# The gradient transposed on TensorE in the head, two spectral pieces a step in the first group, and eight b tiles at the front of pass two

## The chip, the cores and the metric

The kernel runs on one core of a Trainium2 chip. The time is the device time of one execution in microseconds (us), as a median over runs; every run told here is of the fast state. Runs of one kernel on one chip scatter by up to 9 us (the kernel before took 1568.8 to 1577.8 us in 11 runs on one chip), so each comparison uses the runs of the kernel before that were made in the same rounds. Times inside an execution come from its trace, one for each kernel and two for the changed one; the two traces of the changed kernel differ by 1.9 us at the end of pass one and by 2.4 us in pass two, so a difference of that size between two traces proves nothing by itself. Engines: PE is TensorE, ACT is ScalarE, DVE is VectorE, POOL is GpSimd, SP is SyncE, which here only issues transfers. The granted clock of PE is given as a share of full speed.

## The reference, cut to what matters

Forward and backward pass of a gated sum of two branches over x with S = 2048 rows and D = 576 columns (bf16):

```python
g = sigmoid((x * gate_w).sum(-1, keepdims=True))
a = irfft2(rfft2(x) * (w_r + 1j * w_i))              # spectral branch
b = (gelu(x @ w_gate) * (x @ w_up)) @ w_down         # F = 4608
out = g * a + (1 - g) * b
# returned: out and the gradients of x, w_r, w_i, w_gate, w_up, w_down, gate_w for grad_out
```

Both branches read the same x. The gradient `grad_out` is needed in two layouts: natural (rows on partitions, tile `dB`) and transposed (columns on partitions, tile `dOT`).

## The kernel before

It has three stages. The **head** loads x, transposes it on PE chunk by chunk, and does the first two stages of the spectral transform for 16 row tiles. **Pass one** walks through 18 groups of 256 hidden columns, 8 steps each: matmuls H (`z` for the gradient, `xy` for gate and up), elementwise work on ACT and DVE, weight gradients W of the group before, and, in between, "pieces" of the spectral transforms. **Pass two** reads the stored hidden activations back with transposing transfers and computes b and the gradient of x.

The loads stand in one queue, that of SP (`LD`), and so do the stores of the head:

```python
for k in range(4):
    load_x(4 * k)
do_s = [dram.tile([4, P, 5 * P], BF16, name=f"do_s{k}") for k in range(4)]
for k in range(4):
    src = do_v[:, 4 * k:4 * k + 4, :].rearrange("p t d -> t p d")
    LD.dma_start(do_s[k][:, :, 0:D], src)            # staging copy, HBM to HBM
    LD.dma_start(do_s[k][:, :, D:], src[:, :, 512:D])
wts = {0: load_w(0)}
for k in range(4):
    LD.dma_start_transpose(dOT[:, :, 4 * k:4 * k + 4, :]..., do_s[k]...)
...
# second stage of a row tile t
Vt = unit([2, DF], name="Vt")                        # one of 19 shared buffers
V.tensor_copy(Vt[:], vps[:, :, :DF])
LD.dma_start(dst[t], Vt[:])                          # stored on the same queue
```

A step of pass one, and the pace of the pieces (`n` pieces done by the half step `h`; a `gap` in the list of pieces is an empty one, and `Vp` is a tile that the middle pieces load back from what the first ones stored):

```python
fft_until(want(step, 0))        # pieces of the first half; PSUM tile pf, one buffer
pts = H_mm(g, tp)               # z (every second step) and xy
tiles = H_ew1(g, tp, pts)       # ACT: da, q, xb, hu;  DVE: s, s, q, q
fft_until(want(step, 1))        # pieces of the second half
H_sig(tiles)
...
H_ew2(g, tp, tiles)
...
if h <= 2 * NT:                                      # group 0
    n = max(0, 3 * (h - 1) // 2)
```

In pass two `g` and `u` are the two halves of the gradient of x for a row tile (they share an accumulator), `b` is the down projection:

```python
jobs = [("g", t) for t in range(3)] + [("b", t) for t in range(6)] + [("u", t) for t in range(3)] + [("b", 6)]
for t in range(3, T):
    jobs += [("g", t), ("u", t)] + ([("b", t + 4)] if t + 4 < T else [])
...
for i, (kind, t) in enumerate(jobs):
    if i > 1 and wT_loads:
        load_wuT(*wT_loads.pop(0))                   # six transposing loads, jobs 2 to 7
```

## Time and profile before

The time is 1572.4 us. The prediction below shows and reads the profile's lines; this is the summary:

| stretch | from, us | length, us | what the trace shows |
|---|---|---|---|
| head, first part | 0 | 44.5 | PE busy 34.4 |
| hole | 44.5 | 19.1 | PE busy 0.29, ACT 0.64, DVE 0; buffers of Vt wait for their stores |
| head, rest | 63.6 | 14.3 | clock 0.62 of full |
| group 0 | 77.9 | 74.4 | PE busy 53.0 |
| groups 1 to 17 | 152.3 | 973.5 | PE-bound, but one group 6 us longer than its neighbours |
| pass two | 1125.8 | 444.7 | PE-bound, but for the b tiles in front |

The trace's span is 1570.5 us. "First z" below is the first z matmul, the start of group 0; the end of group 0 is z of step 8; pass two begins with the first matmul into `acc`.

### The profile page before, as it was taken

The numbers are of one execution on the slowest core, as the hardware profiler recorded it, in microseconds if no ns is written. First come the engines' busy times: TensorE is split into PE (matmuls) and PEld (weight loads), VectorE is DVE, ScalarE is ACT, GpSimd is POOL, SyncE is SP. The second block draws the span as 40 slices with busy tenths as digits, with TensorE's granted clock in tenths as the row PEclk, the third lists the DMA queues.
The fourth block names the chain that finished last, engine by engine and source line by source line (L and its number), as shares of the span: only waits on it lengthen the run. The fifth ranks groups of instructions, "written<-read, shape, count | busy, mean of one in ns | idle before, by whom it ended". The sixth has DMA issues, their size and how long they took to land.

```text
span 1570.5 us, 30102 instructions
## 1 busy us (share of the span) xinstructions
PE 1482.8 (94%) x11762; PEld 1080.0 (69%) x11886; DVE 823.7 (52%) x2168; ACT 708.8 (45%) x1357; POOL 22.5 (1%) x51
## 2 busy tenths in 40 slices
PE   7377999899999999999999999999998999999998
PEld 5234666566676666677767776766876777777776
DVE  6246767687888887656665665677112212121210
ACT  5145666576666666666666666666000000000000
POOL 0000000000000000000000000000000000000000
PEclk9689999999999999999999999999999999999999
DMA  3642333443544445344334454364999978777873
GB/s 122 156 154 74 104 110 110 144 131 117 149 142 138 132 117 166 98 117 118 101 111 118 121 118 122 102 157 122 266 191 207 207 156 170 156 166 158 172 149 70
DMA packets 518671, 217.47 MB, mean 138 GB/s; under 512 B 320128, under 2 KB 511616, under 8 KB 518528
## 3 DMA queue, kind: packets, MB, share of 16 engines
q1 hardware_dynamic: 515088, 209.80, 54.4%
q0 software_dynamic: 1632, 4.72, 1.1%
q8 instruction: 93, 1.52, 0.4%
q10 hardware_dynamic: 1808, 1.02, 0.2%
q14 instruction: 50, 0.41, 0.1%
HBM read 44.39 MB, written 97.33 MB: 90 GB/s over the span
## 4 chain that ended last, share of the span: by engine, by line
PE 68%; issue 23%; SPq 5%; DVE 1%; ACT 1%; POOL 1%; DMA 1%; POOLq 0%; DVEq 0%; ACTq 0%
PE wps L413 16%; PE xy L330 16%; PE wps L396 9%; PE z L319 8%; PE pf L666 3%; PE acc L870 3%; PE xy L327 2%; PE wps L424 2%; PE acc L912 2%; PE z L323 1%; SPq L246 1%; PE pf L453 1%; SPq L247 1%; SPq L250 1%; PE pf L650 1%
## 5 line engine op out<-in xcount | busy, mean ns | idle before, releaser
L330 PE MATMUL xy<-wgu,xT 128*128 128x512 bf16 x1028 | 257.4, 381 | 13.5 <-issue 10.4
L912 PEld LDWEIGHTS <-pin 128*128 128x128 bf16 x2304 | 225.4, 98 | 58.3 <-DMA pin<-scr 1.6
L413 PEld LDWEIGHTS <-xn 128*128 128x128 bf16 x2304 | 225.2, 98 | 35.5 <-issue 0.2
L330 PEld LDWEIGHTS <-xT 128*128 128x128 bf16 x1152 | 101.3, 98 | 143.5 <-issue 42.4
L341 ACT ACTIVATE da<-z,omg 128x256 bf16<-128x256 f32 x288 | 121.0, 473 | 103.6 <-PE z L323 103.6
L345 DVE TENSOR_SCALAR s<-q 128x512 bf16<-128x512 bf16 x144 | 42.2, 293 | 212.5 <-ACT q L342 212.2
L342 ACT ACTIVATE q<-xy 128x512 bf16<-128x512 f32 x144 | 86.0, 597 | 148.7 <-PE xy L330 148.7
L396 PE MATMUL wps<-dB,A 128*128 128x288 bf16 x1152 | 151.7, 288 | 0.0
L870 PE MATMUL acc<-wd_all,pin 128*128 128x288 bf16 x1152 | 145.3, 288 | 6.5 <-DMA pin<-scr 3.5
L912 PE MATMUL acc<-wuT,pin 128*128 128x288 bf16 x1152 | 143.4, 286 | 1.3 <-DMA pin<-scr 1.3
L319 PE MATMUL z<-wdT,dOT 128*128 128x256 bf16 x1152 | 140.9, 277 | 3.2 <-DVE Vt L475 3.2
L912 PE MATMUL acc<-wgT,pin 128*128 128x288 bf16 x1152 | 143.4, 286 | 0.0
L870 PEld LDWEIGHTS <-pin 128*128 128x128 bf16 x1152 | 113.3, 98 | 36.6 <-DMA pin<-scr 4.3
L396 PEld LDWEIGHTS <-A 128*128 128x128 bf16 x1152 | 113.6, 99 | 33.2
L413 PE MATMUL wps<-dHg,xn 128*128 128x256 bf16 x1152 | 131.7, 273 | 0.0
L413 PE MATMUL wps<-dHu,xn 128*128 128x256 bf16 x1152 | 131.3, 273 | 0.0
L319 PEld LDWEIGHTS <-dOT 128*128 128x128 bf16 x1152 | 114.0, 99 | 19.7 <-issue 3.8
L922 ACT COPY f32t<-acc 128x576 f32<-128x576 f32 x16 | 10.2, 639 | 250.5 <-PE acc L912 250.5
L924 DVE SCALAR_TENSOR_TENSOR f32t<-gwf,dlog,f32t 128x576 f32<-128x576 f32 x16 | 13.1, 818 | 179.7 <-ACT f32t L922 179.7
L353 ACT ACTIVATE om<-s 128x512 bf16<-128x512 bf16 x144 | 91.9, 638 | 15.1 <-DVE s L346 14.9
L354 ACT ACTIVATE s<-s 128x512 bf16<-128x512 bf16 x144 | 90.7, 630 | 4.6
L344 ACT CAST hu<-xy 128x512 bf16<-128x512 f32 x144 | 86.8, 603 | 0.0
(179 smaller groups left out, 1770.7 us busy)
## 6 DMA issues: line engine op xcount, KB each, us to landing
scr<-A SPq DMA_DIRECT2D x144, 128.0 KB
scr<-dHg SPq DMA_DIRECT2D x144, 128.0 KB
scr<-dHu SPq DMA_DIRECT2D x144, 128.0 KB
out_dram<-dw SPq DMA_DIRECT2D x67, 128.0 KB
wd_all<-in_B_w_down_dram SPq DMA_DIRECT2D x3, 1728.0 KB
out_dram<-dwd SPq DMA_DIRECT2D x34, 144.0 KB
scr_p<-Vt SPq DMA_DIRECT2D x32, 144.5 KB
Vp<-scr_p SPq DMA_DIRECT2D x16, 289.0 KB
```

What stands on the lines that cost most here:

```text
L319: nc.tensor.matmul(zt[0][:, t % 2, (t - t0) // 2, :], lhsT=dOT[:, ci, t, :], rhs=wdT[:, ci, :], start=(t < t0 + 2 and ci == 0), stop=False)
L330: nc.tensor.matmul(xy[:, tt, :], lhsT=xT[:, ci, t0 + tt, :], rhs=wgu[:, ci, :], start=False, stop=(ci == 3))
L341: nc.scalar.activation(da[:, tt, :], da_ps[:, tt, :], ACT.Copy, scale=omg32[:, t0 + tt:t0 + tt + 1])
L342: nc.scalar.activation(q[:], hg, ACT.Square)
L344: nc.scalar.copy(hu[:], hu_ps)
L353: nc.scalar.activation(om[:], s[:], ACT.Sigmoid, scale=-2.0 * C_GELU)
L354: nc.scalar.activation(s[:], s[:], ACT.Sigmoid, scale=2.0 * C_GELU)
L396: nc.tensor.matmul(wps[:, :288], lhsT=tl(0, t)[:, fch * P:(fch + 1) * P], rhs=dB[:, t, h * 288:(h + 1) * 288], start=(t == 0), stop=(t == ...
L413: nc.tensor.matmul(wps[:, cc, :], lhsT=xn[:, t, (c0 + cc) * P:(c0 + cc + 1) * P], rhs=tl(k, t), start=(t == 0), stop=(t == T - 1))
L666: nc.tensor.matmul(yps[:, h, :288], lhsT=Z[:, lc, c, :], rhs=tb.At[lc][:, c, h * 288:(h + 1) * 288], start=(n == 0), stop=(n == 5))
L870: nc.tensor.matmul(bps[:, h, :288], lhsT=At[:, r, :], rhs=wd_all[:, fc, h * 288:(h + 1) * 288], start=(fc == 0), stop=(fc == NFC - 1))
L912: nc.tensor.matmul(xps[:, h, :288], lhsT=src[:, r, :], rhs=wT[:, h * 288:(h + 1) * 288], start=(k == 1 and f0 + r == 0), stop=(k == 2 and ...
```

## The change

The intent was to take the gradient's staging and its DMA transposes out of the queue by transposing on PE from `dB`, which pass one needs anyway; to have one spectral piece a half step in group 0; and to give pass two more b tiles before the first u tile needs `wuT`. The diff, cut:

```diff
-    do_s = [dram.tile([4, P, 5 * P], BF16, name=f"do_s{k}") for k in range(4)]
     for k in range(4):
-        src = ...
-        LD.dma_start(do_s[k][:, :, 0:D], src)
-        LD.dma_start(do_s[k][:, :, D:], src[:, :, 512:D])
+        load_do(4 * k)
     wts = {0: load_w(0)}
-    for k in range(4):
-        LD.dma_start_transpose(dOT[...], do_s[k][...])
 ...
-    def x_chunk(t0):
+    def tchunk(src, dst, t0):          # 16 + 8 PE transposes, 3 copies
 ...
         if t % 4 == 2 and t < 14:
-            x_chunk(t + 2)
+            tchunk(xn, xT, t + 2)
+        if t >= 9 and t % 2 == 1:
+            tchunk(dB, dOT, 2 * (t - 9))
 ...
-    fft = at + fg + [gap] * 3 + mid[:-2] + ...
+    fft = at + fg + [gap] * 5 + mid[:-2] + ...
 ...
-    slot0 = 3 * (2 * NT - 1) // 2
+    slot0 = 2 * NT - 1
 ...
-            n = max(0, 3 * (h - 1) // 2)
+            n = max(0, h - 1)
 ...
-        for t0 in range(0, T, 4):      # in early_loads, step 1
-            load_do(t0)
 ...
-    jobs = ... [("b", t) for t in range(6)] + [("u", t) for t in range(3)] + [("b", 6)]
+    jobs = ... [("b", t) for t in range(8)] + [("u", t) for t in range(3)] + [("b", 8)]
     for t in range(3, T):
-        jobs += [("g", t), ("u", t)] + ([("b", t + 4)] if t + 4 < T else [])
+        jobs += [("g", t), ("u", t)] + ([("b", t + 6)] if t + 6 < T else [])
```

More of the change, by code (lines that the diff above doesn't have):

```diff
@@ L242 @@
         load_x(4 * k)
-    do_s = [dram.tile([4, P, 5 * P], BF16, name=f"do_s{k}") for k in range(4)]
     for k in range(4):
-        src = do_v[:, 4 * k:4 * k + 4, :].rearrange("p t d -> t p d")
-        LD.dma_start(do_s[k][:, :, 0:D], src)
-        LD.dma_start(do_s[k][:, :, D:], src[:, :, 512:D])
+        load_do(4 * k)
     wts = {0: load_w(0)}
-    for k in range(4):
-        LD.dma_start_transpose(dOT[:, :, 4 * k:4 * k + 4, :].rearrange("d c t p -> d c (t p)"),
-                               do_s[k][:].rearrange("t p d -> (t p) d"))
     gwb = res.tile([P, D], BF16, name="gwb")
@@ L284, in x_chunk @@
                     if c < 4:
-                        nc.tensor.transpose(tp_[:, 0, j, tt, :], xn[:, t0 + tt, c * P:(c + 1) * P], ident[:])
+                        nc.tensor.transpose(tp_[:, 0, j, tt, :], src[:, t0 + tt, c * P:(c + 1) * P], ident[:])
                     else:
                         for r in (LO, HI):
-                            nc.tensor.transpose(tp_[r, 0, 0, tt, :], xn[:, t0 + tt, 512:D], ident[:])
-            o = xT[:, cs[0]:cs[0] + len(cs), t0:t0 + 4, :]
+                            nc.tensor.transpose(tp_[r, 0, 0, tt, :], src[:, t0 + tt, 512:D], ident[:])
+            o = dst[:, cs[0]:cs[0] + len(cs), t0:t0 + 4, :]
             i = tp_[:, 0, 0:len(cs)]
@@ L687 @@
     build_D(nc, tb, unit, res)
-    x_chunk(0)
+    tchunk(xn, xT, 0)
     run_late(tb)
@@ L711 @@
     mid = mid_units()
-    fft = at + fg + [gap] * 3 + mid[:-2] + [load_At] + pa + mid[-2:] + [gap] * 2 + ia[:-4] + pb + ia[-4:] + ib
+    fft = at + fg + [gap] * 5 + mid[:-2] + [load_At] + pa + mid[-2:] + [gap] * 2 + ia[:-4] + pb + ia[-4:] + ib
     fft_pos = [0]
@@ L809, in pin @@
         return tl
-    jobs = [("g", t) for t in range(3)] + [("b", t) for t in range(6)] + [("u", t) for t in range(3)] + [("b", 6)]
+    jobs = [("g", t) for t in range(3)] + [("b", t) for t in range(8)] + [("u", t) for t in range(3)] + [("b", 8)]
     for t in range(3, T):
-        jobs += [("g", t), ("u", t)] + ([("b", t + 4)] if t + 4 < T else [])
+        jobs += [("g", t), ("u", t)] + ([("b", t + 6)] if t + 6 < T else [])
     seq = [("bgu".index(kind), t, f0) for kind, t in jobs for f0 in range(0, NFC, FCB)]
```

## The prediction

> **What bounds the kernel now.** I read the page first. Its second part, engines in 40 slices, says that PE is at 9 tenths in nearly every slice except the first four, and that its clock was not granted in slices two and three:
>
> ```profile
> PE   7377999899999999999999999999998999999998
> PEclk9689999999999999999999999999999999999999
> ```
>
> A slice is 1570.5/40 = 39.3 us, so whatever is to be gained lies mostly before 157 us. The view of windows (us; busy time and count of each engine; PE clock; DMA share; GB/s) cuts that stretch at its events: head up to the stall, stall, rest of head, first half of group 0, second half, then groups of 8 steps.
>
> ```profile
> 0.00:44.50 44.50, 34.43 (x284) 22.29 (x284) 27.52 (x69) 23.92 (x39) 3.57 (x17) 1.00 0.39 121
> 44.50:63.60 19.10, 0.29 (x3) 0.18 (x3) 0.00 (x0) 0.64 (x1) 0.00 (x0) 0.55 0.92 207
> 63.60:77.90 14.30, 9.85 (x117) 6.21 (x117) 7.11 (x22) 5.24 (x11) 0.00 (x0) 0.62 0.50 110
> 77.90:117.90 40.00, 29.33 (x160) 15.64 (x162) 18.28 (x45) 16.44 (x31) 1.05 (x1) 0.80 0.48 151
> 117.90:152.30 34.40, 23.64 (x165) 13.98 (x165) 22.55 (x59) 18.26 (x35) 0.00 (x0) 1.00 0.23 72
> 205.40:259.30 53.90, 53.16 (x425) 37.75 (x429) 36.95 (x104) 35.66 (x70) 0.00 (x0) 1.00 0.43 123
> 259.30:319.20 59.90, 55.37 (x414) 38.06 (x419) 42.83 (x114) 36.21 (x72) 0.00 (x0) 0.94 0.42 123
> ```
>
> For 19.1 us no engine computes at all; group 0 has PE busy 29.33 of 40.0 and 23.64 of 34.4; the group at 205 is PE-bound; the group at 259 is 6.0 us longer than the one before it. The view of waits names the first hole, and the timeline of the SP queue its cause:
>
> ```profile
> ACT Y L459 <- DMA scr_x<-Vt: 21.5, 1, 21.5
> DVE XR L127 <- DMA scr_x<-Vt: 20.5, 1, 20.5
> ```
>
> ```profile
> 27.07 5.90 SPq L246 DMA_DIRECT2D do_s<-in_grad_out_dram  x1
> 33.02 2.40 SPq L247 DMA_DIRECT2D do_s<-in_grad_out_dram  x1
> 35.46 6.16 SPq L215 DMA_DIRECT2D wgu<-in_B_w_gate_dram  x1
> 47.98 12.20 SPq L250 DMA_TRANSPOSE dOT<-do_s  x4
> 60.28 7.39 SPq L478 DMA_DIRECT2D scr_x<-Vt  x13
> ```
>
> All loads and the stores of the spectral results Vt share this queue in program order. The staging copies, weights and transposes of the gradient hold it until 60.28; thirteen finished Vt tiles keep their buffers (the shared ring of 19), and the next Y and XR have none. PE, at matmul 13 of 16 of the head, stops.
>
> In group 0 the timeline of PE shows what makes a step long (two steps take 135.09 - 117.91 = 17.2 us, with 4 waits of 1.07, 0.85, 2.46 and 0.84 us):
>
> ```profile
> 127.52 1.90 PE L330 MATMUL xy<-wgu,xT 128*128 128x512 bf16 x8
> 129.63 0.29 PE L472 MATMUL pf<-Y,Rt 128*128 128x289 bf16 x1
> ...
> 132.38 1.15 PE L453 MATMUL pf<-Dt,dOT 128*128 128x289 bf16 x8 [2.46 <-DVE Vt L475]
> 134.59 0.28 PE L469 MATMUL pf<-Y,Rt 128*128 128x289 bf16 x1 [0.84 <-ACT Y L461]
> ```
>
> The tile pf has one buffer: a spectral piece cannot start before the one before it has been copied out, and three pieces a step often stand back to back.
>
> **What the Trainium skill says.** "DMA: Bandwidth & Descriptors", Specifications, puts line rate at transfers of 512 B and more. The trace agrees: the copy of the last 64 columns (128 B rows, 64 KB) holds the queue 2.0 to 6.4 us, while the later plain load of the same gradient, 4 x 576 KB in long rows, takes 2.27 us to issue for all four. "TensorE: Matmul & The Clock Gate", the part on the HAM clock gate, says that about 3.4 us of idleness halve the clock and about as much work restores it. It agrees: the granted clock is 0.50 from 48 to 70 us, after the stall began, and in a later dip (108 to 111 us, also 0.50) eight 512-column matmuls take 2.69 us against 1.90. The same page, Part 4, says that a PE transpose ends in PSUM and needs a copy. Here 16 transposes of x take 1.07 us, 8 half ones 0.41, and three copies 0.68, 0.42 and 1.01 us follow.
>
> **Part one, the gradient's transposes.** Removed: 8 staging copies, 4 DMA transposes on the queue. Moved: the four plain loads of dB from step 1 to the start. The queue is then through with loads plus weights (2.0 + 2.3 + some 7 us of issue), and even if it waits for the weight transposes behind 5.6 MB, at the 380 to 407 GB/s that the windows show at 102 to 108 us that is before 20 us. Nine Vt at most have accumulated, so the ring does not fill, and the 19.1 us go, with the slow clock after them. Added: four chunks of 16 + 8 transposes, after t = 9, 11, 13, 15 of the head. Three x chunks of the same size lengthened their interval from 1.82 us (start to start of two L453 groups, such as 20.96 to 22.78) to 4.31 (34.38 to 38.69), 3.58 with 0.7 more in the next two, and so on: I take 2.4 us each. From t = 9, which starts at 32.56 today: 1.82 + 2.4 = 36.8; t = 10 has an x chunk, 4.3: 41.1; t = 11: 45.3; t = 12 with 0.5 for tables: 47.6; t = 13: 51.8; t = 14: 53.6; then 1.4 + 2.4 + 0.6 to the end of the last but one second-stage group: 58.0. From there to the first z matmul it takes 6.1 us today (71.8 to 77.9: table, sigmoid, last Vt), which stays. Group 0 starts at 64.1 instead of 77.9: **-13.8 us**.
>
> **Part two, two pieces per step.** Each half step now has one piece, so the first-stage piece (1.38 us) stands before the step's H matmuls, the second-stage one (0.6 us) after. The latter is behind xy; its copy on DVE follows the four elementwise operations of the step. Today in that position 2.96 us pass from the end of xy (146.6) to the next piece (149.56). So two steps take 2 x (2.96 + 1.38 + 2.3) + 2.3 for z = 15.6 us against 17.2. In the first steps, following the same durations: z of step 2 at 94.2 instead of 97.45, z of step 4 at 112.1 instead of 117.9, then 127.7 and 143.3 instead of 152.27 (on today's clock of events): 9.0 us less. But by step 8 only 15 instead of 22 pieces are done. The seven others, three first-stage (10 x 0.12 = 1.2 us of PE) and four second-stage (4 x 0.12 = 0.49), go into groups that are PE-bound: +5.6. Net **-3.4 us**.
>
> **Part three, where the pieces fall later.** The group at 259 us has this:
>
> ```profile
> PE pf L542 <- DMA Vp<-scr_x: 3.8, 1, 3.8
> ```
>
> Its load was queued at 283.45 behind the next weight set (276.6 to 283.4), and the clock fell to 0.50 afterwards. Total price 59.9 - 53.9 = 6.0 us. The pace formula puts the piece that issues this load at group 3, step 2, just behind the weight loads of step 1. With 15 pieces at group 0's end, 176 slots in all (two more gaps) and 161/15 per group, it moves to group 4, step 0, and its user to step 1, first half, before the weights. One step, 6.7 us, against 3.7 us until the queue is free of the last step's stores plus about 3 us of transfer: nearly hidden. I count **-5.5 us**.
>
> **Part four, eight b tiles in front.** g0, g1 and g2 hold three of the four accumulators, so leading b tiles share the fourth, and each start waits for the copy: the trace has 3.0 us in 4 such waits, 0.77 each. Two more leading tiles give two more, of which one coincides with a wait for pin (1.3 us) that today stands before u0: **+0.8 us**. The wuT loads are issued at jobs 2 to 7 in both orders, so the shortage of pin of 3.5 us before b5 stays.
>
> Sum: 1572.4 - 13.8 - 3.4 - 5.5 + 0.8 = 1550.5. Clock drops in the thinner group 0 (idle stretches of 2.5 us with 0.6 us of work beside them) may take one or two us back: I say **1552 us**.
>
> **Rivals.** (a) The head becomes bound by evacuation or by late dB: the chunks of dO meet the table builds. Summed for t = 9 to 11, DVE has 3 x 0.76 + 3 x 1.1 + 1.75 = 7.3 us and PE 10.0, so PE stays the bound; but the three PSUM buffers rotate, and if a chunk costs 4 us rather than 2.4, the head gives back 6.4: 1558. (b) Group 0 is no shorter, as its thin PE load lets the clock fall: 9.0 us of gain vanish while 5.6 are added later: 1561. For it speaks that the clock fell at 94 and 107 us today; against, that the same 2.46 us gap at 112 to 115 and again at 130 left it at 1.00. (c) The wait for Vp survives at its new place: 1557. (d) Pass two gains: DMA catches up before u0, removing 1.3 us and no more; 1550.
>
> **Range and chances.** The stall's removal is nearly certain and is worth 11 to 16 us; (b) and (c) each have perhaps one chance in four. That gives 1543 to 1562 for 8 in 10. Faster by over 2% means under 1540.9, for which everything must go better than worked out: 0.07. Slower by over 2% would need a new stall of 50 us: 0.01. Within 2%: 0.92.
>
> **What would show it.** Right: no wait of an engine for scr_x<-Vt over 1 us; first z near 64 us; two steps of group 0 near 15.6 us; z of step 8 near 130; no wait of PE for Vp over 1 us and no group of 59.9 us before the inverse pieces; six or seven waits of 0.77 us for the accumulator in pass two, same wait for pin. Wrong: a granted clock near 0.5 through group 0, PE waiting for the PSUM copies of the dO chunks, or a new wait in the groups that took over the seven pieces.

## The result

The changed kernel took 1544.94 us (1542.3 to 1547.2, 4 runs) against 1571.44 us for the kernel before in the same rounds. The ratio is 0.9831, 95% interval 0.9808 to 0.9855. A ratio here is the mean time of one kernel's fast runs over that of the other's of the same rounds, so it is not quite the ratio of the medians quoted. The result is faster by 1.7%, inside the range given (and within the 2% to which the prediction gave 0.92), 7 us below the 1552 us named. A second measurement in later rounds gave 1548.0 against 1574.1 us, ratio 0.9837. All outputs are right.

The view of windows of the changed kernel, cut at the same events as that of the kernel before (start:end in us, length, busy time and count of PE, PE weight loads, DVE, ACT and POOL, then the granted PE clock, DMA share, GB/s):

```profile
0.00:44.50 44.50, 34.44 (x313) 23.20 (x314) 29.46 (x73) 25.82 (x41) 3.57 (x17) 1.00 0.50 163
44.50:60.70 16.20, 12.15 (x185) 9.07 (x183) 9.34 (x27) 7.83 (x14) 0.00 (x0) 0.94 0.15 48
60.70:92.30 31.60, 23.58 (x143) 13.08 (x145) 18.18 (x49) 15.69 (x30) 1.05 (x1) 0.87 0.37 112
92.30:126.40 34.10, 23.95 (x136) 12.23 (x137) 21.77 (x60) 17.39 (x32) 0.00 (x0) 0.86 0.21 65
```

The hole is gone: the head ends at 60.7 instead of 77.9 us. Group 0 takes 65.7 instead of 74.4 us, although its granted clock is 0.87 and 0.86 in the two halves. The timeline of its SP queue shows why the hole is gone (start, length, engine, source line, operation, tiles, count):

```profile
2.85 2.17 SPq L239 DMA_DIRECT2D dB<-in_grad_out_dram  x4
...
19.21 0.50 SPq L220 DMA_DIRECT2D wdT<-wdT  x1
19.81 41.23 SPq L472 DMA_DIRECT2D scr_x<-Vt  x16
```

The stores of Vt start at 19.8 us and follow the computation; before, the first of them was issued at 60.28 us. The head's PE timeline shows what a chunk of the gradient costs:

```profile
45.73 1.15 PE L447 MATMUL fx<-Dt,xT 128*128 128x289 bf16 x8
...
47.04 1.07 PE L279 MATMUL tp<-ident,dB 128*128 128x128 bf16 x16
48.04 0.41 PE L282 MATMUL tp<-ident,dB 128*64 128x128 bf16 x8
48.76 0.28 PE L463 MATMUL fx<-Y,Rt 128*128 128x289 bf16 x1 [0.31 <-ACT dOT L286]
...
49.26 1.15 PE L447 MATMUL fx<-Dt,xT 128*128 128x289 bf16 x8
...
51.08 1.15 PE L447 MATMUL fx<-Dt,xT 128*128 128x289 bf16 x8
```

With a chunk the interval between two first-stage groups is 3.53 us (45.73 to 49.26), without one 1.82 (49.26 to 51.08): 1.7 us a chunk, of which 1.41 us is PE's own time and 0.31 us the wait for a copy. The view of waits names what PE still waits for (total, times, longest, in us):

```profile
PE pf L447 <- DVE Vt L469: 13.1, 6, 2.5
PE acc L864 <- ACT f32t L869: 4.5, 6, 0.8
PE z L313 <- DVE Vt L469: 3.8, 1, 3.8
PE acc L864 <- DMA pin<-scr: 2.3, 1, 2.3
```

No wait for `Vp<-scr_x` is left. The largest wait in group 0 is now that for the copy of Vt: five times 2.46 us, and 0.8 us once after it. The saving runs like this through the trace: 17.1 us at the first z, 25.9 at the end of group 0, 24.5 at the start of pass two, 25.2 at the end.

### The profile page after: what moved, and what is told of

Same layout as the page of the kernel before. It is cut to its first block, busy times and chain, and to the rows that moved or that the text cites. A ratio compares the mean times of both kernels' runs of the same rounds, so it can differ in the third digit from the quotient of the medians.

```text
span 1545.3 us, 30301 instructions
## 1 busy us (share of the span) xinstructions
PE 1483.3 (96%) x11857; PEld 1082.0 (70%) x11982; DVE 825.9 (53%) x2176; ACT 711.7 (46%) x1361; POOL 22.5 (1%) x51
## 3 DMA queue, kind: packets, MB, share of 16 engines
q1 hardware_dynamic: 500592, 204.56, 53.3%
## 4 chain that ended last, share of the span: by engine, by line
PE 84%; issue 10%; DVE 2%; DMA 2%; ACT 2%; SPq 0%; POOL 0%; POOLq 0%; ACTq 0%; DVEq 0%
PE wps L407 16%; PE xy L324 16%; PE acc L906 10%; PE wps L390 9%; PE z L313 8%; PE acc L864 8%; PE pf L660 3%; PE xy L321 2%; PE wps L418 2%; PE z L317 2%; PE pf L447 1%; PE pf L644 1%; PE pf L646 1%; DMA wgu<-in_B_w_gate_dram 1%; PE fx L447 1%
## 5 line engine op out<-in xcount | busy, mean ns | idle before, releaser
L313 PEld LDWEIGHTS <-dOT 128*128 128x128 bf16 x1152 | 113.7, 99 | 20.4 <-issue 4.2
L916 ACT COPY f32t<-acc 128x576 f32<-128x576 f32 x16 | 10.2, 638 | 249.1 <-PE acc L906 249.1
L918 DVE SCALAR_TENSOR_TENSOR f32t<-gwf,dlog,f32t 128x576 f32<-128x576 f32 x16 | 13.1, 818 | 187.6 <-ACT f32t L916 187.6
L869 ACT COPY f32t<-acc 128x576 f32<-128x576 f32 x16 | 10.2, 638 | 167.4 <-PE acc L864 158.3
```

The source lines that it names most:

```text
L313: nc.tensor.matmul(zt[0][:, t % 2, (t - t0) // 2, :], lhsT=dOT[:, ci, t, :], rhs=wdT[:, ci, :], start=(t < t0 + 2 and ci == 0), stop=False)
```

## The experiments

This table has the places in each trace, in us, and the ratio to the kernel before in the same rounds. Pass two is the span less its start.

| kernel | first z | group 0 | start of pass two | pass two | span | ratio (95%) |
|---|---|---|---|---|---|---|
| before | 77.9 | 74.4 | 1125.8 | 444.7 | 1570.5 | 1 |
| changed | 60.8 | 65.7 | 1101.3 | 444.0 | 1545.3 | 0.9831 (0.9808 to 0.9855) |
| e12_changed_again | 60.8 | 64.0 | 1099.3 | 446.4 | 1545.7 | 0.9837 (0.9820 to 0.9854) |
| e1_transpose_only | 61.4 | 74.4 | 1109.4 | 447.0 | 1556.4 | 0.9908 (0.9891 to 0.9924) |
| e2_pace_only | 77.1 | 66.1 | 1118.1 | 443.0 | 1561.1 | 0.9944 (0.9929 to 0.9959) |
| e3_jobs_only | 76.9 | 74.4 | 1125.0 | 445.0 | 1570.0 | 1.0020 (1.0003 to 1.0037) |
| e4_three_gaps | 60.8 | 64.3 | 1107.5 | 447.2 | 1554.7 | 0.9895 (0.9880 to 0.9910) |
| e5_stores_other_queue | 60.0 | 79.0 | 1113.0 | 442.2 | 1555.2 | 0.9909 (0.9888 to 0.9929) |
| e6_chunks_twice | 67.5 | 65.9 | 1108.3 | 445.5 | 1553.8 | 0.9891 (0.9869 to 0.9912) |
| e7_last_piece_first | 57.1 | 65.2 | 1096.7 | 445.2 | 1541.9 | 0.9813 (0.9793 to 0.9833) |
| e8_copy_before_ew | 60.7 | 55.1 | 1092.0 | 443.4 | 1535.3 | 0.9785 (0.9764 to 0.9805) |
| e10_spread_wuT | 61.2 | 66.2 | 1102.4 | 440.8 | 1543.2 | 0.9819 (0.9806 to 0.9833) |
| e9_all | 57.3 | 53.3 | 1085.1 | 441.7 | 1526.8 | 0.9718 (0.9704 to 0.9731) |
| e11_two_g | 57.5 | 53.3 | 1085.4 | 443.3 | 1528.6 | 0.9732 (0.9718 to 0.9747) |

The theory to be tested: the change is worth the hole plus the shorter group 0 plus the Vp wait, less the moved pieces, and each of these stands by itself. Rivals: the parts share one cause (the low clock after the hole), or the transposes on PE were not what removed the hole.

### One part alone

**e1_transpose_only** undoes the pace, the gaps and the job order (parts two, three and four of the prediction) in the changed kernel:

```diff
-    fft = at + fg + [gap] * 5 + mid[:-2] + ...
+    fft = at + fg + [gap] * 3 + mid[:-2] + ...
-    slot0 = 2 * NT - 1
+    slot0 = 3 * (2 * NT - 1) // 2
-            n = max(0, h - 1)
+            n = max(0, 3 * (h - 1) // 2)
-    (new job order)
+    (old job order)
```

> The changed kernel with the old pace (three pieces a step, three gaps) and the old job order, so part one alone. If the parts simply add: first z at 60.8 us as in the changed kernel, group 0 as long as before (74.4 us from z of step 0 to z of step 8), the wait for Vp with its low clock back (a group of about 60 us), pass two as before; in all 17 us less than before, 1554 us. Rival: the slow clock that the stall left behind had lengthened group 0, so that group 0 is shorter by itself once the stall is gone (under 70 us) and the pace change adds nothing: 1549 us or less.

Measured: 1558.6 us against 1573.7. First z at 61.4, group 0 of 74.4 us to the tenth, a wait of 4.0 us for Vp and a group of 60.0 us between groups of 52.6 and 53.9 (the groups after group 0 are cut at the first matmul of L418, here and in e4). The wait in its view:

```profile
PE pf L536 <- DMA Vp<-scr_x: 4.0, 1, 4.0
```

Pass one ends 16.4 us earlier. The rival of the slow clock falls: group 0 does not get shorter by itself. The time was 4 us above what was expected, of which 3 us are pass two (447.0 us, against 444.0 in the changed kernel's first trace); more on that below.

**e2_pace_only** is the kernel before with the pace and the gaps alone:

```diff
-    fft = at + fg + [gap] * 3 + mid[:-2] + ...
+    fft = at + fg + [gap] * 5 + mid[:-2] + ...
-    slot0 = 3 * (2 * NT - 1) // 2
+    slot0 = 2 * NT - 1
-            n = max(0, 3 * (h - 1) // 2)
+            n = max(0, h - 1)
```

> The kernel before with two pieces a step and five gaps, nothing else: part two with its consequence for Vp. If the parts add: the stall of 19 us stays, group 0 is 65.7 instead of 74.4 us, the seven later pieces cost about 5.6 us, the wait for Vp (6.0 us with the clock) is gone: 7 to 9 us less, 1563 to 1564 us. Rival: the shorter group 0 is paid back in full by the later pieces and the Vp wait only moves: within 2 us of the kernel before.

Measured: 1563.0 us against 1573.7. Group 0 is 66.1 us, the Vp wait is gone, pass one ends 7.7 us earlier. From the end of group 0 to pass two it takes 975.0 us, against 973.6 in e1, which has the wait for Vp. That wait costs 60.0 - 53.9 = 6.1 us, so the seven later pieces cost 975.0 - (973.6 - 6.1) = 7.5 us, not 5.6. With 16.4 from e1 the two parts give 24.1 us at the start of pass two, where the changed kernel has 24.5 (26.5 in its second trace): within the scatter they add.

**e3_jobs_only** puts the new job order into the kernel before.

```diff
-    jobs = ... [("b", t) for t in range(6)] ... [("b", 6)]    and ("b", t + 4)
+    jobs = ... [("b", t) for t in range(8)] ... [("b", 8)]    and ("b", t + 6)
```

> The kernel before with eight b tiles leading pass two, nothing else. Prediction on record: two more waits of 0.77 us for the shared accumulator, one of them hidden: 0.8 us longer. Rival, after the traces: the shortage of pin becomes smaller (2.3 instead of 3.5 us) and the 1.3 us before u0 goes, so 0.7 us shorter. Either is near the noise; the waits in the trace tell: where the pin wait stands and how long it is.

Measured: 1576.0 us against 1573.7, ratio 1.0020; pass two 445.0 us. Its interval, 1.0003 to 1.0037, is 0.5 to 5.8 us longer: it shows no gain, agrees with the 0.8 us and speaks against the rival's 0.7 us less. The waits named beforehand:

```profile
PE acc L870 <- DMA pin<-scr: 4.3, 2, 2.6
```

They are 1.7 us before b5 and 2.6 before b6, with none before u0; the kernel before has 3.5 before b5 and 1.3 before u0. So the wait for pin moved and is 0.5 us shorter in all, while the waits for the accumulator grew from 3.0 to 3.8 us. In the traces with the old order pass two takes 444.7, 447.0, 443.0 and 442.2 us, in the seven with the new order and the old wuT loads 444.0, 446.4, 445.0, 447.2, 445.5, 445.2 and 443.4: the means differ by 1.0 us, in favour of the old order, and the scatter is larger. That the new order gains anything is not shown.

### The gaps and the wait for Vp

**e4_three_gaps** is the changed kernel with two gaps less:

```diff
-    fft = at + fg + [gap] * 5 + mid[:-2] + ...
+    fft = at + fg + [gap] * 3 + mid[:-2] + ...
```

> The changed kernel with three gaps instead of five before the middle pieces. By the pace formula the piece that loads the second Vp pair then stands at group 3, step 7, first half, and its user in the second half of the same step, about 3.5 us later. Theory: the load, held behind the stores of the step before, lands some 7 us after its place, so PE waits about 3 us and the clock may fall: 3 to 6 us longer than the changed kernel, 1548 to 1551 us. Rival: the gaps are immaterial, what moved the load was the lower slot count at group 0's end: 1545 us, no wait for Vp.

Measured: 1556.9 us against 1573.7, 9 to 10 us more than the changed kernel by the ratios (0.9895 against 0.9831 and 0.9837). Its view of waits, and its SP queue just before:

```profile
PE pf L536 <- DMA Vp<-scr_x: 5.9, 1, 5.9
```

```profile
288.04 0.53 SPq L422 DMA_DIRECT2D out_dram<-dwt  x1
288.61 0.59 SPq L423 DMA_DIRECT2D out_dram<-dwt  x1
289.25 0.58 SPq L509 DMA_DIRECT2D Vp<-scr_x  x1
```

The load stands behind the output stores of the step and is issued at 289.25, 7.9 us after its piece began on PE (281.37). PE waits 5.9 us, and that group takes 62.7 us where the next takes 54.4. The pass ends 6.2 and 8.2 us later than in the two traces of the changed kernel. So the two extra gaps are worth some 8 us: they are not padding but what moves the load away from its user. The direction was expected, the size (3 to 6 us) was too small. Pass two was 3.2 us longer than in the changed kernel's first trace, within its scatter.

### What removed the hole

**e5_stores_other_queue** leaves the staging and the DMA transposes of the kernel before and issues only the head's stores from POOL:

```diff
-                LD.dma_start(dst[t], Vt[:])
+                (ST if src is xT else LD).dma_start(dst[t], Vt[:])
```

> The kernel before, with the head's stores of Vt issued from the idle POOL queue instead of SP; staging, DMA transposes and all else stay. Theory: the stall was the order of one queue, so the 19 us hole goes although no transfer is removed; the first z then comes at 56 to 62 us, held by the head or by the transposes of the gradient (issued from 48 us on): 16 to 20 us less than before, 1551 to 1555 us, about what PE transposes alone give. Rival: the DMA engines, not the queue, were full; then the stores land no earlier, the hole shrinks by less than 6 us, and the time stays above 1565 us.

Measured: 1558.1 us against 1572.0, ratio 0.9909, the same as e1. No engine waits for a store of Vt (scr_x<-Vt) any more; the first z comes at 60.0 us. But PE is through with the head at 50.4 us and then waits for the transposed gradient. From the view of waits and the SP queue:

```profile
PE z L319 <- DMA dOT<-do_s: 9.6, 1, 9.6
```

```profile
54.21 12.32 SPq L250 DMA_TRANSPOSE dOT<-do_s  x4
```

This settles the cause of the hole: it was the order in one queue, with finished tiles waiting behind loads, and no transfer had to be removed to close it. It also shows how little the PE transposes add. They take away the wait of 9.6 us, but bring four chunks of PE work (1.7 us each) and leave a wait of 3.8 us for the copy of Vt in its place: the first z comes at 60.0 us here, at 60.8 in the changed kernel and at 61.4 in e1, and e1 and e5 have the same ratio. A gain from transposing on PE, beyond the removal of the hole, is not shown. Group 0 was longer here, 79.0 us at a mean clock of 0.82, against 74.4 at 0.89; why the clock was lower more often was not tested. Its 4.6 us more cover the 3 us by which the time misses the expected 1551 to 1555.

**e6_chunks_twice** does each gradient chunk twice in the changed kernel:

```diff
             tchunk(dB, dOT, 2 * (t - 9))
+            tchunk(dB, dOT, 2 * (t - 9))
```

> The changed kernel with each of the four gradient chunks transposed and copied twice (same result). It measures what a chunk costs the head. Prediction on record: 2.4 us each, 9.6 us in all, 1554.5 us. From the trace of the changed kernel: 1.7 us each, 6.8 us, 1551.7 us, first z at 67.6 us. If it is the copies that bind when chunks crowd, more than 2.4 each.

Measured: first z at 67.52 instead of 60.75 us, so 6.77/4 = 1.69 us a chunk. Pass one ends 7.1 us later. The value, 2.4, was wrong, and the copies do not bind even when chunks crowd. The time, 1555.4 us, has 1.5 us more of pass two in it.

### What still holds group 0, and a faster kernel

**e7_last_piece_first** moves one line of the changed kernel's head:

```diff
+    x2[T - 1]()
     build_B(nc, tb, unit, res)
     run_late(tb)
     gate()
-    x2[T - 1]()
```

> The changed kernel with the head's last second-stage piece moved before the table build and the gate. Today the first z waits 3.8 us for the copy of that piece, which stands on DVE behind the gate's chain, and the clock is then at half for some 6 us. Theory: z starts right after the gate's matmuls, at 56.5 to 57.5 instead of 60.75 us, and warm: 4 to 6 us less, 1539 to 1541 us. Rival: the elementwise work then waits for the gate's result, and step 0 ends as late as today: under 1.5 us.

Measured: the first z at 57.05 us without a wait, and warm:

```profile
57.05 1.91 PE L313 MATMUL z<-wdT,dOT 128*128 128x256 bf16 x16
```

The same 16 matmuls took 3.57 us in the changed kernel. Pass one ends 4.5 us earlier, as expected; the time was 1542.9 us, above the 1541 expected, again by pass two (445.2).

**e8_copy_before_ew** has DVE copy the second-half piece of steps 3 to 7 before its elementwise operations:

```diff
+            if 3 <= step < NT:
+                fft_until(want(step, 1))
             tiles = H_ew1(g, tp, pts)
             fft_until(want(step, 1))
```

> The changed kernel with the second-half piece of steps 3 to 7 emitted before the elementwise operations of its step, so that its copy stands before them on DVE; PE's order is unchanged. Theory: the 2.46 us waits for Vt in group 0 shrink to about 1.1 us, five of them: 6 to 8 us less with fewer clock drops, 1537 to 1539 us. Rival: the delayed elementwise work holds the next step instead and group 0 stays at 65.7 us: within 1.5 us of the changed kernel.

Measured: 1538.6 us against 1572.0; group 0 takes 55.1 instead of 65.7 us, pass one ends 9.3 us earlier, and the clock in group 0 is 0.93 instead of 0.86. The largest wait of group 0:

```profile
PE pf L447 <- DVE Vt L469: 7.3, 6, 2.5
```

It was 13.1 us in the same 6 waits. Of the five in group 0, three are now 0.85 us, one 1.46 and one still 2.49. So a copy that stood behind four short operations of its own engine lengthened the steps. The waits themselves account for 5.8 of the 10.6 us; the rest goes with PE's busy time in the group, 43.26 instead of 47.54 us at the higher clock. A second buffer for pf, the other way to remove this wait, was not tried.

**e10_spread_wuT** spreads the six wuT loads over the longer lead, in the changed kernel:

```diff
-            if i > 1 and wT_loads:
+            if i in (2, 4, 5, 7, 8, 10) and wT_loads:
```

> The changed kernel with the six loads of wuT issued at jobs 2, 4, 5, 7, 8 and 10 instead of 2 to 7, as the longer lead of b tiles allows. Theory: in the lead the queue of DMA transposes is the bound; the shortage of pin near b6 (2.3 us, then half clock for one tile, 1.7 us more) comes from the wuT loads standing close together, so it goes or halves: pass two 440 to 442 us, 2 to 4 us less than the changed kernel. Rival: the shortage is the sum of all transfers of the lead and only moves: within 1 us.

**e12_changed_again** is the changed kernel once more, beside it.

> The changed kernel once more, on the chip of the three runs beside it, to compare them with. 1542 to 1548 us; pass one ends at 1101.3 us as in its first trace, within 1 us, and what scatters is pass two (the traces so far have 442 to 447 us for it, whatever the job order).

Measured: e10 1544.5 us, the changed kernel 1548.0 us. In the timeline of PE, the seventh b tile of the changed kernel in this run (first line) and of e10 (second):

```profile
1188.42 10.36 PE L864 MATMUL acc<-wd_all,pin 128*128 128x288 bf16 x72 [4.46 <-DMA pin<-scr]
```

```profile
1187.27 8.98 PE L864 MATMUL acc<-wd_all,pin 128*128 128x288 bf16 x72 [0.77 <-ACT f32t L869]
```

The wait for pin is 4.46 us in this run (2.33 in the first trace of the same kernel), and the tile after it runs partly at half clock: 10.36 instead of 8.98 us. With the loads spread both are gone and pass two takes 440.8 instead of 446.4 us (443.4 to 447.2 in the seven traces with the loads together). The mean times differ by 2.8 us, though the ranges of four runs touch (1543.8 to 1545.0, and 1544.1 to 1548.9). Pass one of e12 ended at 1099.3 us, 1.9 us from the first trace and outside the 1 us expected: in group 0 the clock dropped at other places.

**e9_all** joins the edits of e7, e8 and e10.

> The changed kernel with three edits at once: last piece before the gate, copy before the elementwise operations in group 0, wuT loads spread. Alone in their traces the first two ended pass one 4.5 and 9.3 us earlier. If they add: pass one ends at 1087 to 1089 us, and with the spread loads 1527 to 1531 us in all. Rival: both had their gain partly from the same low clock at the start of group 0; then 1090 to 1092 us and 1533 us or more.

Measured: 1528.6 us against 1574.1, ratio 0.9718: 2.8% faster than the kernel before and some 19 us faster than the changed kernel beside it (1548.0). Pass one ends at 1085.1 us: 1101.3 - 4.5 - 9.3 = 1087.5 was the sum, so nothing of the gains is lost; that it is 2.4 us below, and 1.9 us below the expected 1087, is near the scatter of 1.9 us between the traces of the changed kernel. The clock is 1.00 in the second half of group 0. PE is busy for 97% of the span.

**e11_two_g** is e9 with two g tiles instead of three at the front of pass two, and loads at jobs 2, 4, 5, 6, 8 and 9:

```diff
-    jobs = [("g", t) for t in range(3)] + [b 0 to 7] + [("u", t) for t in range(3)] + [("b", 8)]
+    jobs = [("g", t) for t in range(2)] + [b 0 to 7] + [("u", t) for t in range(2)] + [("b", 8)]
```

> The kernel with the three edits, and two g tiles instead of three in front, so that the leading b tiles have two accumulators to alternate between (wuT loads at jobs 2, 4, 5, 6, 8 and 9). Theory: the waits of 0.77 us for the copy of the accumulator (six, 4.5 us) go, if the transposes of pin keep up: 3 to 4 us less than the kernel with the three edits. Rival: the lead is bound by the DMA transposes, and waits for pin take the place of those removed: within 1 us, or longer by a clock drop.

Measured: 1530.6 us, 2 us more than e9. The waits for the accumulator, seven of 0.7 to 0.8 us in e9's trace, are gone, and in their place the view of waits has:

```profile
PE acc L866 <- DMA pin<-scr: 3.2, 2, 2.0
PE acc L908 <- DMA pin<-scr: 2.9, 2, 2.7
```

The rival holds: with the accumulator's waits gone, the transposing transfers set the pace of the lead. That the waits for the accumulator had given them time fits, but the wuT loads stand elsewhere too, and the two edits were not run apart.

## Why the prediction was right or wrong, point by point

The working is in the prediction; here is what each term measured, in us at the trace of the changed kernel.

| term | predicted | measured | from |
|---|---|---|---|
| head and hole, first z | -13.8 | -17.1 | 77.9 to 60.8 |
| group 0 | -9.0 | -8.7 | 74.4 to 65.7 |
| seven moved pieces | +5.6 | +7.5 | e1 and e2 |
| wait for Vp | -5.5 | -6.1 | e1 |
| pass two | +0.8 | -0.7 | 444.7 to 444.0, within the scatter |
| clock drops in group 0 | +1.5 | in the group 0 line | |
| sum | -20.4 | -25.1 | span 25.2 |

The mechanism of **part one** was right: the hole was a queue in the wrong order (e5), its removal is worth what e1 shows, and the stores flow from 19.8 us, "before 20 us". Its size was off by one mis-sized term: "I take 2.4 us each" for a gradient chunk measured 1.7 (e6 gives 1.69), and four chunks make 2.8 of the 3.3 us by which the head came out too long. The prediction's own second interval had the right size, 3.58 - 1.82 = 1.76 us; its 2.4 adds delays that stand near the x chunks. In the trace of the kernel before, the chunk in the interval of 4.31 us has two waits inside it, 0.56 us for a copy of Vt and 0.28 for Y, where the gradient chunk shown above has one of 0.31. Why the x chunks meet more waits was not tested. The rest of the head's difference is in the start of tile 9 (32.13 instead of 32.56).

**Part two** was right in mechanism and in its total. By its account steps 2 and 3 took 17.9 us (94.2 to 112.1, at a low clock) and the two pairs after them 15.6 each. The trace has 15.5, 16.5 and 17.6: the clock dropped later than assumed, the rival (b) in a mild form, and the differences nearly cancel. That the total came out so close is in part luck. The timeline of PE in the changed kernel, a second-stage piece and the first-stage pieces after it:

```profile
96.78 0.29 PE L466 MATMUL pf<-Y,Rt 128*128 128x289 bf16 x1
99.53 1.85 PE L447 MATMUL pf<-Dt,dOT 128*128 128x289 bf16 x8 [2.46 <-DVE Vt L469]
...
107.49 1.15 PE L447 MATMUL pf<-Dt,dOT 128*128 128x289 bf16 x8 [2.46 <-DVE Vt L469]
```

The same eight matmuls after the same wait of 2.46 us take 1.85 us at 99.53 and 1.15 at 107.49. The seven pieces cost 7.5 instead of 5.6 us; what the other 1.9 are was not found, and stays open.

**Part three** was right: the load moved to where the pace formula put it, and no wait was left. e4 shows that the two gaps do this, and that a full step between load and user is enough: with half a step the wait is 5.9 us.

**Part four** was wrong in its details. The sentence that the shortage of pin of 3.5 us before b5 "stays" failed: in the changed kernel's first trace it stood before b6 and was 2.3 us, in the second 4.5 us. Its size is a matter of the run more than of the order (e3 and the list of pass-two times), and it can be removed by spreading the wuT loads (e10). Two more waits of 0.77 us did come and the wait of 1.3 us before u0 went, as written.

The **rivals**: (a) falls by e6, since a chunk costs less and not more; (b) holds in part; (c) falls in the changed kernel and is what e4 brings back; (d) is within the scatter. The result lies 5 us beyond the sum of the terms and within the range, chiefly because one repeated term was taken 0.7 us too large.

One **reading** of the prediction does not hold. It sets the skill's 512 B for line rate beside the time for which copies of 128 B rows hold the queue, and says that the trace agrees. The 576 KB copies beside them have rows of 1152 B and hold the queue longer, 5.9 to 6.3 us in three of four, and the plain load of wgu behind them holds it 6.16 us where the changed kernel has 0.51. So the hold seems to follow what stands ahead in the queue and not the row length; no run here shows the 512 B. The sums do not use it.

## What to carry to other kernels

A transfer queue works in program order here: a store that frees a buffer should not be issued behind loads that nobody waits for yet, and moving it to an idle queue tells cheaply whether order or bandwidth is at fault (here -14 us by one word). When a tile has one PSUM buffer, look at where its copy stands in the program of the copying engine and not only at that engine's load: DVE was busy for 40 of the 65.7 us of group 0, and moving the copy ahead of four short operations gave 9 us, waits and clock together. Small pacing constants, such as two gaps more, can decide whether a load stands a step or half a step before its user, so they should be tried by themselves before they are called padding.

## What the Trainium skill lacked or had wrong

- "TensorE: Matmul & The Clock Gate", section "Why this matters for your kernels", advises no PE-idle gaps over about 3 us between bursts. That is not enough: in group 0 of the changed kernel a gap of 2.46 us (97.07 to 99.53) was followed by half clock (0.50 from 100 to 102 us), while one of the same length (105.03 to 107.49) left it at 1.00 until 116 us. The group's length differed between two runs of the same kernel (65.7 and 64.0 us). The page's section "A second HAM failure mode: psum-queue depth-cycling" does say that frequent short idles make the clock swing, but gives no length for them.
- The same page, Part 4, gives about 390 ns for one transpose in isolation and about 275 ns in a kernel, and no rate for a row of them. Here one record is 219 ns, but 16 back to back take 1.07 us, 67 ns each, and a chunk of 24 with its copies mostly hidden costs 1.69 us.
- No page that I found says how long a transfer of many rows holds its issuing queue, or how this grows with what stands ahead. Here three of four HBM-to-HBM copies of 576 KB held SP for 5.9 to 6.3 us, the first of them 0.88 us, and a load of wgu behind them 6.16 us, against 0.51 us behind plain loads in the changed kernel. Four loads of 576 KB in 4608 B rows were issued in 2.17 us together. The DMA share of the first 44.5 us was 0.39 in the kernel before.
